# Moving one stage six steps later, reordering four loads, and giving the last stores more buffers and a second queue

## The chip, the cores and the metric

The kernel runs on one core of a Trainium2 chip. The metric is the device time of one execution in microseconds (us), as the median of several runs. A profile (a trace of one execution) exists of every kernel named here; its span is about 2 us shorter than the time of the same run. Engines: PE is the matmul engine, ACT, DVE and POOL (GpSimd) are the elementwise engines, SP only issues DMAs here.

## The reference

A filter in the frequency domain, then a gated feed-forward network (FFN) on the result:

```python
# x (8, 3008, 256); filt_r, filt_i (1505, 256); w_gate, w_val (256, 1536); w_out (1536, 256)
X = np.fft.rfft(x, axis=1)
y = np.fft.irfft(X * (filt_r + 1j * filt_i)[None], n=3008, axis=1)
t = y.reshape(24064, 256)
out = (np.maximum(t @ w_gate, 0) * (t @ w_val)) @ w_out
```

## The kernel before

The Fourier transform is factored, 3008 = 94 x 32, and done by matmuls in stages for each of eight batches:

- stage A: `psA` from x, written as `asb` to DRAM (`Abuf`, four stores), read back in another order as `at` (four loads);
- stage B: `psX` from `at`, times the filter, `psD`, written to DRAM (`Dbuf`), read back as `dC` (eight loads, z = 0 to 7; call them D loads);
- stage C: `psY` from `dC` into `yT`, the input of the FFN.

The FFN has 47 blocks of 512 tokens with 12 steps each. A step makes `psV` and `psG` (four matmuls, 0.86 us together) and, for the block before, a third of a 128-row tile of `psO` (four matmuls, 0.43 us), so about 1.30 us. The stages of the next batch are put between the steps, at step numbers that the program gives. Batch 0 has nothing to hide behind; it is the prologue, about 63 us.

```python
def load_at(b, c):                                    # SP queue
    ...
    nc.sync.dma_start(ats[b][32 * c:32 * c + 32], ... Abuf[b] ...)

def load_d(b, z0=0, z1=NZ):                           # SP queue
    for z in range(z0, z1):
        dC = sb.tile([NROW, 4, D], BF16, tag="dC", bufs=12)
        nc.sync.dma_start(dC, ... Dbuf[b] ...)
...
    last = blk == NB - 1                              # o_part: psO and the output
    if s in (5, 11) or last and s % 3 == 2:
        t0 = t if last else t - 1
        osb = fs.tile([128, 2, D], FP32, tag="osb", bufs=3)
        nc.scalar.copy(osb[...], psO[...])
        for tt in range(t0, t + 1):
            for (o, b, n2, n1, w) in runs(blk * W + tt * 128, 128):
                nc.sync.dma_start(_ap(out, ..., [[N2 * D, w], [1, D]]), osb[o:o + w, tt % 2])
...
for f in items_b(0, amid): f()                        # end of the prologue
load_d(0, 0, 2)
... # WvT, WgT, WoT: the rest of the FFN's weights, by POOL
for i in range(8): next(early)()                      # stage A of batch 1, 12 of its 16 parts now done
for h in range(2): item_c(0, h)
load_d(0, 2)                                          # six more D loads
...
C_AT = (8, 10)                                        # stage C of the next block in each block
for b in range(1, B):
    s0, sb0 = (0, 13) if b == 1 else ...              # first step of stage A, of stage B
    ...
        at_step(... if b > 1 else 4, lambda b=b, c=c: load_at(b, c))
    for i, f in enumerate(items_b(b)):
        at_step(sb0 + 2 * i, f)
    at_step(sb0 + 27, lambda b=b: load_d(b))
```

A tile of 128 token rows is scattered in DRAM: `runs` cuts it where a row of the 94 x 32 grid ends, so its store is two or three DMAs of, say, 94 and 34 rows of 1 KB each.

## Time and profile before

985.33 us, median of three runs (983.27 to 986.04); the profiled span is 982.2 us.

The profile's page, engines' busy time and the chain of waits (the work that ended last, followed backwards):

```profile
PE 951.0 (97%) x6020; PEld 565.2 (58%) x6020; DVE 544.9 (55%) x823; ACT 526.7 (54%) x940; POOL 42.9 (4%) x76
PE 91%; DMA 5%; SPq 1%; ACT 0%; issue 0%; DVE 0%; POOL 0%; ACTq 0%; POOLq 0%
```

PE bounds this kernel. A change that leaves PE's instructions alone can win only its holes, so the next view is what PE waited for. Columns: who waited, the producer, total us, how often, the longest.

```profile
PE psX L274 <- DMA at<-Abuf: 16.3, 3, 8.2
...
PE psO L373 <- ACT osb L379: 2.5, 2, 2.0
...
PE psG L355 <- DMA WgT<-in_moe_w_gate_dram: 1.3, 1, 1.3
```

Of the 16.3 us, 8.2 are in the prologue and 0.8 near 338 us. The rest is one hole of 7.33 us, seen in PE's timeline (start, duration, what; in brackets the idle time before it and who ended it):

```profile
81.63 0.60 PE L373 MATMUL psO<-WoT,prod 128*128 128x256 bf16 x4
89.55 0.61 PE L274 MATMUL psX<-at,F 128*128 128x256 bf16 x2 [7.33 <-DMA at<-Abuf]
89.95 1.06 PE L355 MATMUL psV<-yT,WvT 128*128 128x512 bf16 x2
```

The psV after the hole takes 1.06 us instead of 0.59. The view of stretches of time says why: the last three numbers of each line are the granted clock, the DMA share and GB/s, and the clock is 0.50. (The DMA share is the summed time of the packets over that of 16 engines. Packets overlap, so it can pass 1.)

```profile
82.00:89.50 7.50, 0.23 (x3) 0.00 (x0) 0.69 (x1) 0.00 (x0) 0.00 (x0) 0.76 0.91 141
89.50:92.50 3.00, 2.95 (x10) 1.49 (x11) 1.81 (x3) 0.59 (x1) 2.42 (x6) 0.50 0.38 98
```

What the `at` load waited for is on SP's timeline: the last Abuf store of stage A leaves at 71.67, behind six D loads.

```profile
63.18 8.39 SPq L317 DMA_DIRECT2D dC<-Dbuf  x6
71.67 1.60 SPq L247 DMA_DIRECT2D Abuf<-asb  x1
73.38 8.78 SPq L261 DMA_DIRECT2D at<-Abuf  x4
```

Last, the tail in the chain of waits: a store holds an `osb` buffer, ACT waits for it, PE waits for ACT and then runs its last 12 matmuls at half clock.

```profile
968.76 3.94 DMA out_dram<-osb
...
972.88 0.38 ACT osb L379
973.26 0.04 issue
973.30 2.69 PE psO L373 x12
```

The end of the run in the view of stretches matters later. But for one short copy on ACT only the DMA engines work, and they only little: a share of 0.14 or 0.15 is about two of 16, at about 50 GB/s.

```profile
976.20:978.20 2.00, 0.00 (x0) 0.00 (x0) 0.00 (x0) 0.23 (x1) 0.00 (x0) 0.50 0.14 48
978.20:980.20 2.00, 0.00 (x0) 0.00 (x0) 0.00 (x0) 0.00 (x0) 0.00 (x0) 0.50 0.15 51
```

### The profile page before, as it was taken

What the parts mean: (1) busy time and instruction counts of PE and PEld (TensorE: products, weight loads), DVE (VectorE), ACT (ScalarE), POOL (GpSimd) and SP (SyncE); (2) the same over time, 40 slices, a digit from 0 to 9 for tenths busy, and PEclk for the clock granted to TensorE, in tenths of its full rate; (3) what the DMA queues carried; (4) which work ended last, traced back from release to release, by engine and by line L of the source; (5) the groups of instructions that cost most, each with busy time, mean ns of one, the idle gap of its engine ahead of it and who ended that gap; (6) DMA issues with size and microseconds to landing.
All of it is one profiled execution on the core that took longest, in us unless ns stands there. A gap on an engine that the chain in (4) does not pass through costs nothing.

```text
span 982.2 us, 16279 instructions
## 1 busy us (share of the span) xinstructions
PE 951.0 (97%) x6020; PEld 565.2 (58%) x6020; DVE 544.9 (55%) x823; ACT 526.7 (54%) x940; POOL 42.9 (4%) x76
## 2 busy tenths in 40 slices
PE   8696999999999999999999999999999999999996
PEld 3343666556664566556665566655666556666664
DVE  2635865348653576536854377543775348655552
ACT  4463555555555555555555555555555555555552
POOL 4221000010000100001000010000100000000000
PEclk9798999999999999999999999999999999999998
DMA  9989241243243442345241362423614241241111
GB/s 261 241 223 236 85 117 38 78 127 144 79 98 94 123 148 80 73 102 199 64 125 46 94 199 80 113 56 102 189 57 113 71 107 44 80 98 34 33 33 44
DMA packets 94432, 106.29 MB, mean 108 GB/s; under 512 B 7796, under 2 KB 84724, under 8 KB 92660
## 3 DMA queue, kind: packets, MB, share of 16 engines
q1 hardware_dynamic: 87520, 80.03, 30.5%
q0 software_dynamic: 6240, 22.71, 7.8%
q10 hardware_dynamic: 592, 2.51, 0.7%
q8 instruction: 47, 0.77, 0.4%
q14 instruction: 33, 0.27, 0.1%
HBM read 59.32 MB, written 49.81 MB: 111 GB/s over the span
## 4 chain that ended last, share of the span: by engine, by line
PE 91%; DMA 5%; SPq 1%; ACT 0%; issue 0%; DVE 0%; POOL 0%; ACTq 0%; POOLq 0%
PE psO L373 24%; PE psV L355 24%; PE psG L355 24%; PE psA L242 10%; DMA Abuf<-asb 3%; PE psX L274 2%; PE psY L339 2%; PE psD L294 2%; PE psD L293 2%; DMA at<-Abuf 2%; SPq L317 1%; PE psJ L392 1%; DMA out_dram<-osb 0%; ACT asb L245 0%; POOL uu L281 0%
## 5 line engine op out<-in xcount | busy, mean ns | idle before, releaser
L360 DVE SCALAR_TENSOR_TENSOR prod<-psG,vsb 128x512 bf16<-128x512 f32 x564 | 390.1, 692 | 370.4 <-ACT vsb L358 358.4
L358 ACT CAST vsb<-psV 128x512 bf16<-128x512 f32 x564 | 331.2, 587 | 223.3 <-PE psV L355 192.5
L373 PE MATMUL psO<-WoT,prod 128*128 128x256 bf16 x2256 | 338.5, 274 | 2.5 <-ACT osb L379 2.5
L355 PE MATMUL psG<-yT,WgT 128*128 128x512 bf16 x1128 | 335.8, 379 | 1.3 <-DMA WgT<-in_moe_w_gate_dram 1.3
L355 PE MATMUL psV<-yT,WvT 128*128 128x512 bf16 x1128 | 336.2, 379 | 0.8 <-ACT yT L344 0.6
L373 PEld LDWEIGHTS <-prod 128*128 128x128 bf16 x2256 | 221.4, 98 | 147.1 <-issue 3.4
L355 PEld LDWEIGHTS <-WgT 128*128 128x128 bf16 x1128 | 110.0, 98 | 135.8 <-DMA WgT<-in_moe_w_gate_dram 1.8
L355 PEld LDWEIGHTS <-WvT 128*128 128x128 bf16 x1128 | 104.4, 98 | 59.9 <-issue 49.7
L242 PE MATMUL psA<-XF,WA 128*96 128x512 f32 x256 | 129.5, 592 | 0.0
L245 ACT CAST asb<-psA 96x512 bf16<-96x512 f32 x128 | 74.2, 582 | 102.2 <-PE psA L242 97.7
L296 ACT CAST dsb<-psD 128x512 bf16<-128x512 f32 x96 | 56.1, 587 | 52.6 <-PE psD L294 51.1
L277 DVE TENSOR_TENSOR tt<-psX,Ftr 128x512 bf16<-128x512 f32 x96 | 65.4, 682 | 16.4 <-PE psX L274 15.9
L379 ACT COPY osb<-psO 128x512 f32<-128x512 f32 (+1 forms) x96 | 55.4, 577 | 33.3 <-PE psO L373 27.8
L283 DVE TENSOR_TENSOR uu<-psX,Fti 128x512 bf16<-128x512 f32 x90 | 61.3, 681 | 0.0
L274 PE MATMUL psX<-at,F 128*128 128x256 bf16 x192 | 38.1, 283 | 16.3 <-DMA at<-Abuf 16.3
L294 PE MATMUL psD<-uu,I2u 128*128 128x256 bf16 x192 | 48.2, 278 | 1.6 <-POOL uu L281 1.5
L293 PE MATMUL psD<-tt,I2t 128*128 128x256 bf16 x192 | 48.4, 278 | 0.0
L339 PEld LDWEIGHTS <-dC 96*128 96x128 bf16 x604 | 34.6, 97 | 13.2 <-issue 11.1
L346 DVE CAST yT<-psY 128x512 bf16<-128x512 f32 x47 | 32.1, 684 | 16.4 <-PE psY L339 16.4
L242 PEld LDWEIGHTS psA<-XF,WA 128*96 128x96 f32 x256 | 35.1, 163 | 9.3 <-ACT asb L245 4.0
L344 ACT CAST yT<-psY 128x512 bf16<-128x512 f32 x47 | 27.5, 586 | 19.6 <-PE psY L339 19.5
L339 PE MATMUL psY<-M,dC 96*128 96x94 bf16 (+18 forms) x604 | 37.5, 198 | 0.0
(45 smaller groups left out, 154.9 us busy)
## 6 DMA issues: line engine op xcount, KB each, us to landing
XF<-in_x_dram POOLq DMA_DIRECT2D x34, 512.0 KB, 6.2
Abuf<-asb SPq DMA_DIRECT2D x32, 384.0 KB
at<-Abuf SPq DMA_DIRECT2D x32, 384.0 KB
dC<-Dbuf SPq DMA_DIRECT2D x64, 192.0 KB
Dbuf<-dsb SPq DMA_DIRECT2D x31, 384.0 KB
out_dram<-osb SPq DMA_DIRECT2D x72, 94.0 KB
XF<-in_x_dram SPq DMA_DIRECT2D x8, 512.0 KB
tabs<-dft_tab ACTq DMA_DIRECT2D x2, 576.0 KB
```

The costliest lines, as they stand in the source:

```text
L242: nc.tensor.matmul(psA[0:NROW], WA[:, :NROW], XF[c * NC2 // NX2][:, o:o + 512], start=True, stop=True)
L245: nc.scalar.copy(dst, psA[0:NROW])
L274: nc.tensor.matmul(psX[:, i], F2[:, g + i, :], at[:, g + i, :], start=True, stop=True)
L277: nc.vector.tensor_tensor(tt, psX, Ftr[:, g:g + 2, :], op=ALU.mult)
L283: nc.vector.tensor_tensor(uu, psX, Fti[:, g:g + 2, :], op=ALU.mult)
L293: nc.tensor.matmul(psD[:, i], I2t[:, g + i, :], tt[:, i], start=True, stop=False)
L294: nc.tensor.matmul(psD[:, i], I2u[:, g + i, :], uu[:, i], start=False, stop=True)
L339: nc.tensor.matmul(psY[:, o:o + w], dCs[b, n2 // 4][:, n2 % 4, h * 128:(h + 1) * 128], M1[:, n1:n1 + w], start=True, stop=True)
L355: nc.tensor.matmul(pt[:, :W], w[:, h, ft * 128:(ft + 1) * 128], yt[:, h, :], start=(h == 0), stop=(h == 1))
L358: nc.scalar.copy(vsb, psV[:, :W])
L360: nc.vector.scalar_tensor_tensor(prod, in0=psG[:, :W], scalar=0.0, in1=vsb, op0=ALU.max, op1=ALU.mult)
L373: nc.tensor.matmul(psO[:, t % 2], prods[ft][:, t * 128:(t + 1) * 128], WoT[:, ft, :], start=(ft == 0), stop=(ft == NFT - 1))
```

## The change

The intent: stage B of batch 1 starts when its data are there; the D loads that are not needed yet leave the road to the Abuf store and the `at` loads; the tail no longer waits for an output buffer; two engines issue the last stores.

```diff
-                st["dsb"] = sb.tile([128, GC, D], BF16, tag="dsb", bufs=5, name="dsb")
+                st["dsb"] = sb.tile([128, GC, D], BF16, tag="dsb", bufs=4, name="dsb")
...
-            osb = fs.tile([128, 2, D], FP32, tag="osb", bufs=3)
+            osb = fs.tile([128, 2, D], FP32, tag="osb", bufs=5)
...
-                for (o, b, n2, n1, w) in runs(blk * W + tt * 128, 128):
-                    nc.sync.dma_start(_ap(out, ...), osb[o:o + w, tt % 2])
+                for i, (o, b, n2, n1, w) in enumerate(runs(blk * W + tt * 128, 128)):
+                    eng = nc.scalar if last and i == 1 else nc.sync
+                    eng.dma_start(_ap(out, ...), osb[o:o + w, tt % 2])
...
-    load_d(0, 2)
+    load_d(0, 2, 4)
...
+    for s, z in ((9, 4), (14, 6)):
+        at_step(s, lambda z=z: load_d(0, z, z + 2))
     C_AT = (8, 10)
     for b in range(1, B):
-        s0, sb0 = (0, 13) if b == 1 else (end - 54, end - 30 | 1)
+        s0, sb0 = (0, 19) if b == 1 else (end - 54, end - 30 | 1)
...
-            at_step(s0 + n - 10 + 4 * c if b > 1 else 4, lambda b=b, c=c: load_at(b, c))
+            at_step(s0 + n - 10 + 4 * c if b > 1 else 5, lambda b=b, c=c: load_at(b, c))
```

More of the change, by code (lines that the diff above doesn't have):

```diff
@@ L377, in o_part @@
             t0 = t if last else t - 1
-            osb = fs.tile([128, 2, D], FP32, tag="osb", bufs=3)
+            osb = fs.tile([128, 2, D], FP32, tag="osb", bufs=5)
             nc.scalar.copy(osb[:, t0 % 2:t % 2 + 1], psO[:, t0 % 2:t % 2 + 1])
             for tt in range(t0, t + 1):
-                for (o, b, n2, n1, w) in runs(blk * W + tt * 128, 128):
-                    nc.sync.dma_start(_ap(out, (b * S + n1 * N2 + n2) * D, [[N2 * D, w], [1, D]]),
-                                      osb[o:o + w, tt % 2])
+                for i, (o, b, n2, n1, w) in enumerate(runs(blk * W + tt * 128, 128)):
+                    eng = nc.scalar if last and i == 1 else nc.sync
+                    eng.dma_start(_ap(out, (b * S + n1 * N2 + n2) * D, [[N2 * D, w], [1, D]]),
+                                  osb[o:o + w, tt % 2])
     junk = pro.tile([128, 512], BF16, tag="junk", bufs=1)
```

## The prediction

> **What bounds the kernel now.** The page gives PE 951.0 of 982.2 us busy (97%), and the chain of waits is 91% PE. From 92.5 to 966 us PE is full but for 0.79 us near 338, so only PE's holes can be won. PE's waits and timeline place those that the change can touch:
>
> 1. A hole of 7.33 us, 82.2 to 89.55: psX waits for `at`, the last quarter of batch 1's stage A. SP issues in order: six D loads of batch 0 hold it from 63.18 to 71.57 us, so the last Abuf store, whose ACT copy ended at 71.0, goes out at 71.67, lands after 9.91 us (DMA share 0.9 to 1.0), and its `at` load takes 7.86 us more. A later batch has 7.7 + 4.3 us there and a stall of 0.79 us.
> 2. After the hole the granted clock is 0.50 from 89.5 to 92.5; that costs 1.5 us. The Trainium skill (TensorE: Matmul & The Clock Gate, "The HAM clock gate") has half rate after an idle window of about 3.4 us; the trace agrees.
> 3. 1.29 us at 71 where psG waits for WgT, which shares the DMA engines with the D loads.
> 4. The tail: psO of the last tile waits 2.04 us for the osb copy before it, which waits for an output DMA (3.94 us) as all three osb buffers are in use. Then its 12 matmuls take 2.57 us at half clock instead of 1.3.
>
> **What the change does.** Only two D loads (0.39 MB, not 1.18 MB) stand before the last Abuf store; the order listing shows the other four behind the `at` loads on SP. Stage B starts 6 steps later, 6 x 1.30 = 7.8 us. PE's instructions are the same. Five osb buffers remove the tail wait. The second piece of each last tile is issued by ACT, about 0.3 us each as on SP (estimate), between copies 1.3 us apart.
>
> **Sum.** 0.79 MB less at the 205 GB/s of 55 to 95 us is 3.8 us, so `at` lands at 85 to 86 us. PE reaches its first psX at 88.7 to 90. Item 1 vanishes: -7.3, item 2 with it: -1.5. WgT comes earlier: -1.0. Tail: last psO ends 3.1 us sooner, parallel issue 0.3. Total -13.2.
>
> New waits: z=4 of batch 0 is needed by psY at step 20, about 1.5 us after stage B starts, and is issued behind the last `at` load; I expect it at 87 to 88, a margin of 2 to 3 us. Batch 1's D loads come at step 46 for use at step 56; other batches live with 8 steps. Four dsb buffers: batch 0's fifth use takes the first one again, stored at 45 and wanted at 55; no or a short ACT wait. I allow +0.7 for these.
>
> 985.3 - 13.2 + 0.7 = 972.8 us; range 969.5 to 977.5. Faster by over 2% (under 965.6) 0.02, within 2% 0.97, slower 0.01.
>
> **Right if:** psX <- at falls from 16.3 us to about 9 (8.15 in the prologue stays), the clock is 1.0 through 80 to 95, the pair Abuf and `at` near 70 us shrinks or leaves the chain, psO <- osb copy falls from 2.5 to about 0.5, span near 970.
>
> **Wrong if:** `at` still lands after 90 us because Abuf's 9.9 us is congestion by weights, not D loads; psY waits for dC at steps 20 or 56; ACT's DMA issues cost over 1 us each; dsb reuse stalls the prologue; or the final store's landing, not its issue, grows.

## The result, and the profile after

976.29 us, median of four runs (975.31 to 976.92), against 985.35 us (the three runs of before above and one more). The ratio of the mean time of the changed kernel's runs to that of the kernel before in the same rounds is 0.9911, 95% interval 0.9894 to 0.9928 (so it is not quite the ratio of the medians). The time was inside the predicted range, 3.5 us above the predicted 972.8.

PE's waits after. The 0.5 in the osb line is the longest; the other at<-Abuf wait, of 1.4 us, is near 331 us.

```profile
PE psX L274 <- DMA at<-Abuf: 9.3, 2, 7.9
...
PE psG L355 <- DMA WgT<-in_moe_w_gate_dram: 2.2, 1, 2.2
...
PE psO L373 <- ACT osb L379: 0.9, 2, 0.5
```

The hole is gone, and so is the half clock after it. In the timeline of PE psX follows psO without a gap, and the same stretches of time are at clock 1.00:

```profile
89.83 0.60 PE L373 MATMUL psO<-WoT,prod 128*128 128x256 bf16 x4
90.26 0.38 PE L274 MATMUL psX<-at,F 128*128 128x256 bf16 x2
```

```profile
82.00:89.50 7.50, 7.45 (x47) 4.60 (x47) 3.98 (x6) 3.80 (x7) 1.77 (x5) 1.00 0.94 166
89.50:92.50 3.00, 3.00 (x27) 1.94 (x25) 2.45 (x5) 1.44 (x3) 1.57 (x4) 1.00 1.07 361
```

SP's timeline after: the Abuf store leaves 1.1 us sooner, as soon as its data are there, with two D loads before it and four behind the `at` loads.

```profile
62.71 1.13 SPq L317 DMA_DIRECT2D dC<-Dbuf  x2
70.56 0.31 SPq L247 DMA_DIRECT2D Abuf<-asb  x1
70.97 7.45 SPq L261 DMA_DIRECT2D at<-Abuf  x4
78.47 6.50 SPq L317 DMA_DIRECT2D dC<-Dbuf  x4
```

The tail is another matter. ACT's timeline after: the copies (COPY osb) and the stores that ACT issues. The copy of 963.30 is done at 963.67, but its store goes out at 964.71; the last copy is done at 965.60, its store goes out at 967.08.

```profile
963.30 0.37 ACT L379 COPY osb<-psO 128x256 f32<-128x256 f32 x1 [0.94 <-PE psO L373]
964.71 0.33 ACTq L383 DMA_DIRECT2D out_dram<-osb  x1
965.23 0.37 ACT L379 COPY osb<-psO 128x256 f32<-128x256 f32 x1 [1.56 <-DMA out_dram<-osb]
967.08 0.24 ACTq L383 DMA_DIRECT2D out_dram<-osb  x1
```

The chain of waits names what the first of the two waited for: a store that SP issued at 960.04 and that landed 4.59 us later.

```profile
960.04 4.59 DMA out_dram<-osb
964.63 0.02 issue
964.66 0.02 ACTq L383
```

And the end of the run is as empty as before, DMA share 0.12 to 0.19:

```profile
968.90:970.90 2.00, 0.00 (x0) 0.00 (x0) 0.00 (x0) 0.00 (x0) 0.00 (x0) 0.68 0.19 63
970.90:972.90 2.00, 0.00 (x0) 0.00 (x0) 0.00 (x0) 0.00 (x0) 0.00 (x0) 0.50 0.12 43
```

Cutting both profiled runs at three events that both have (read off PE's timeline) says where the time went:

| stretch | before, us | after, us | difference |
|---|---|---|---|
| start to the first psV (prologue) | 63.33 | 62.87 | -0.46 |
| first psV to the last psG | 902.34 | 894.81 | -7.53 |
| last psG to the end of the last psO | 10.31 | 7.52 | -2.79 |
| end of the last psO to the end | 6.22 | 9.70 | +3.48 |
| span | 982.2 | 974.9 | -7.3 |

The whole tail, from the last psG on, went from 16.53 to 17.22 us. PE finished 2.8 us sooner, and the wait for the stores took it back. (The profiled runs differ by 7.4 us in time, 984.35 and 976.92; the medians by 9.1. The profiled run of after was the slowest of its four. The total PE busy time is not compared: 110 of 6020 matmul records are missing in the second trace.)

Two questions were put to the chip. Which of the early parts, the delay or the order of the D loads, closed the hole? And why did the tail give nothing?

### The profile page after: what moved, and what is told of

It reads as the page before. It is cut to its first block, busy times and chain, and to the rows that moved or that the text cites. A ratio compares the mean times of both kernels' runs of the same rounds, so it can differ in the third digit from the quotient of the medians. Undisturbed runs are those within 1.5% of the kernel's fastest.

```text
span 974.9 us, 16167 instructions
## 1 busy us (share of the span) xinstructions
PE 942.0 (97%) x5910; PEld 564.1 (58%) x6020; DVE 544.3 (56%) x823; ACT 526.7 (54%) x940; POOL 43.0 (4%) x76
## 4 chain that ended last, share of the span: by engine, by line
PE 89%; DMA 5%; ACT 1%; DVE 1%; issue 1%; POOL 0%; ACTq 0%; SPq 0%; POOLq 0%
PE psG L355 24%; PE psO L373 24%; PE psV L355 23%; PE psA L242 9%; DMA Abuf<-asb 2%; PE psX L274 2%; PE psD L294 2%; PE psD L293 2%; PE psY L339 2%; DMA WgT<-in_moe_w_gate_dram 1%; DMA at<-Abuf 1%; DVE prod L360 1%; ACT vsb L358 1%; PE psJ L393 1%; DMA out_dram<-osb 1%
## 5 line engine op out<-in xcount | busy, mean ns | idle before, releaser
L355 PE MATMUL psG<-yT,WgT 128*128 128x512 bf16 x1096 | 328.4, 379 | 5.8 <-DMA WgT<-in_moe_w_gate_dram 2.2
L355 PE MATMUL psV<-yT,WvT 128*128 128x512 bf16 x1051 | 319.0, 379 | 1.6 <-ACT yT L344 0.6
L339 PEld LDWEIGHTS <-dC 96*128 96x128 bf16 x604 | 34.5, 97 | 13.2 <-issue 10.8
```

Source lines behind the costliest of these rows:

```text
L339: nc.tensor.matmul(psY[:, o:o + w], dCs[b, n2 // 4][:, n2 % 4, h * 128:(h + 1) * 128], M1[:, n1:n1 + w], start=True, stop=True)
L355: nc.tensor.matmul(pt[:, :W], w[:, h, ft * 128:(ft + 1) * 128], yt[:, h, :], start=(h == 0), stop=(h == 1))
```

## The experiments

Each was timed against the kernel before in the same rounds. All were correct. The columns "FFN" (first psV to last psG), "PE's end" (last psG to the end of the last psO) and "stores" (from there to the end) are read from each profile as in the table above; "tail" is the sum of the last two. The medians of before in the same rounds were 985.31 us (e1, e2, e3, e9), 984.94 (e4, e6, e7, e8) and 984.93 (g1, g2, g3, f1).

| run | median us | ratio to before | FFN | PE's end | stores | tail |
|---|---|---|---|---|---|---|
| before | 985.33 | 1 | 902.34 | 10.31 | 6.22 | 16.53 |
| after | 976.29 | 0.9911 | 894.81 | 7.52 | 9.70 | 17.22 |
| e1_late_only | 975.26 | 0.9898 | 892.96 | 10.73 | 6.50 | 17.23 |
| e2_dorder_only | 982.66 | 0.9972 | 900.24 | 9.06 | 7.62 | 16.68 |
| e3_no_tail | 975.93 | 0.9902 | 893.78 | 9.49 | 7.66 | 17.15 |
| e9_weights_split | 976.88 | 0.9909 | 894.39 | 7.51 | 9.68 | 17.19 |
| e4_one_queue | 974.64 | 0.9888 | 893.10 | 7.51 | 9.04 | 16.55 |
| e6_split_one_queue | 972.79 | 0.9870 | 893.19 | 7.51 | 6.66 | 14.17 |
| e7_split_two_queues | 973.30 | 0.9875 | 893.20 | 10.61 | 4.19 | 14.80 |
| e8_pool_queue | 973.20 | 0.9875 | 893.54 | 7.51 | 6.91 | 14.42 |
| g1_after_again | 976.22 | 0.9903 | 893.40 | 7.52 | 9.72 | 17.24 |
| g2_late_again | 975.89 | 0.9904 | 893.22 | 9.53 | 7.57 | 17.10 |
| g3_one_queue_again | 974.69 | 0.9896 | 892.73 | 7.51 | 8.97 | 16.48 |
| f1_late_split | 971.41 | 0.9856 | 893.66 | 7.51 | 5.74 | 13.25 |

The 95% intervals are about plus or minus 0.0016 wide (0.0020 for f1_late_split), 1.6 us. Differences below that rest on the traces, where a stretch of the tail repeats within 0.1 us for the same code of the changed kernel (17.22 and 17.24; 16.55 and 16.48).

### e1_late_only: the delay alone

```diff
# against before
-        s0, sb0 = (0, 13) if b == 1 else ...
+        s0, sb0 = (0, 19) if b == 1 else ...
```

> Before with stage B of batch 1 six steps later and nothing else. Theory L (the delay alone closes the hole, since the at load of before lands at 89.5 us and PE reaches its psX at about 90): psX waits for at no more than 0.5 us near 90, the clock stays 1.0 through 80 to 95, about 976.5 us (985.3 less 7.3 less 1.5). Theory O (the order of the D loads is needed too, as the prediction had it): a hole of 2 us or more is left, 979 us or more.

975.26 us. (What the program counts from the first step of stage B moves with it: batch 1's D loads and batch 2's loads of x.) PE's waits show no hole at batch 1: at<-Abuf is 8.3 us in all, of which 7.5 are in the prologue and 0.8 at a later batch. `at` is there by 88.70 us, when POOL, which waits for the same data, goes on; PE reaches its psX at 89.08, with no idle time before it:

```profile
88.70 0.18 POOL L226 CAST scr<-at 32x8 f32<-32x8 bf16 x1 [27.01 <-DMA at<-Abuf]
89.08 0.38 PE L274 MATMUL psX<-at,F 128*128 128x256 bf16 x2
```

Theory L holds. The time is as good as the whole change's, with the six D loads still in the way, though with only 0.4 us to spare (0.3 in the second trace of this kernel, g2). In the changed kernel POOL goes on at 87.28 and PE reaches psX at 90.26: the new order of the D loads bought about 2.6 us of margin, but no time.

### e2_dorder_only: the order alone

```diff
# against before
-    load_d(0, 2)
+    load_d(0, 2, 4)
+    for s, z in ((9, 4), (14, 6)):
+        at_step(s, lambda z=z: load_d(0, z, z + 2))
-            ... if b > 1 else 4, lambda b=b, c=c: load_at(b, c))
+            ... if b > 1 else 5, lambda b=b, c=c: load_at(b, c))
```

> Before with four D loads moved behind the at loads and nothing else. The prediction had at land 3.8 us earlier: hole of 3.5 us left, about 981.5 us. The trace of after has at 2.3 us earlier (87.2 instead of 89.5): hole of about 5 us, 983 us, clock still falling to half after it. If D loads were all of the congestion: hole under 2 us, under 979 us.

982.66 us, 2.8 us less than before by the ratio (0.0028 of 985). PE's timeline still has the hole, 2.15 us shorter, and the slow psV after it:

```profile
82.21 0.60 PE L373 MATMUL psO<-WoT,prod 128*128 128x256 bf16 x4
87.99 0.59 PE L274 MATMUL psX<-at,F 128*128 128x256 bf16 x2 [5.18 <-DMA at<-Abuf]
88.37 1.06 PE L355 MATMUL psV<-yT,WvT 128*128 128x512 bf16 x2
```

So 0.79 MB of D loads out of the way brings `at` about 2.2 us sooner, not the 3.8 that bytes over mean rate gave. (That counts from the first psV, which is 0.55 us later in this trace; on the trace's own clock it is 1.6.) The DMA engines stay as busy as before (share 1.10 at 64 to 66 us and 1.26 at 70 to 72, against 1.03 and 1.26), with POOL's weight loads and SP's loads and stores; that these are what holds up the rest of the path is argued, not shown.

### e3_no_tail: both early parts without the tail part

```diff
# against after
-                st["dsb"] = ... bufs=4
+                st["dsb"] = ... bufs=5
-            osb = ... bufs=5
+            osb = ... bufs=3
-                    eng = nc.scalar if last and i == 1 else nc.sync
+                    eng = nc.sync
```

> After without its tail part (three osb buffers, all stores on SP, five dsb buffers). The prediction had the tail worth 3.4 us: this would take about 979.7 us. The theory from the trace of after (last psO to the end grew by about as much as PE gained): tail worth 0 to 1 us, this 975.5 to 977.3 us, and from the last psG to the end of the span 16.5 us as before.

975.93 us, within the expected range: the tail part of the change was worth nothing. Its tail is 17.15 us, a little over the expected 16.5. The tail of this code (three buffers, SP alone) varies between 16.5 and 17.2 us in five traces (before, e1, e2, e3, g2); the split between PE's end and the stores varies more, 9.1 to 10.7 against 6.2 to 7.7. Most of the difference in PE's end is the clock of its last 12 matmuls: they took 2.7 us at half clock in before and e1, and 1.47 us at full clock in e2, e3 and g2. PE may end early or late, and the end of the run hardly moves.

### e9_weights_split: the weights in two column ranges

```diff
# against after
-    load_vg(DFF // 3, DFF)
+    load_vg(DFF // 3, DFF // 2)
+    load_vg(DFF // 2, DFF)
```

> After with the second load of WvT and WgT cut into two column ranges, the earlier needed first. Theory W (psG of step 4 waits because a whole 0.5 MB WvT load stands before its own columns): the wait of 2.2 us at 70 to 72 vanishes or falls below 0.5, and the time by about 2 us, to 974.2. Rival (the DMA engines are saturated and whatever is asked for comes at 72): the wait stays between 1.5 and 3 us, the time within 1 us of after, or the shorter pieces (256 columns) cost more than they gain and later weights are waited for.

976.88 us: no gain, as the rival had it. PE's waits show the wait for WgT at 1.0 us and a new one of 1.3 us of psO for WoT, which comes later now:

```profile
PE psO L373 <- DMA WoT<-in_moe_w_out_dram: 1.3, 1, 1.3
PE psG L355 <- DMA WgT<-in_moe_w_gate_dram: 1.0, 1, 1.0
```

The 2.2 us of the first profile of the changed kernel were a chance: the same kernel again (g1) waited 1.3 us, and other kernels with the same loads between 0.5 and 1.3.

### e4_one_queue: all stores on SP

```diff
# against after
-                    eng = nc.scalar if last and i == 1 else nc.sync
+                    eng = nc.sync
```

> After with all stores on SP (five osb buffers stay). Theory T (the tail ends when stores of few rows in parallel have landed; who issues them does not matter): from last psG to the end within 1 us of after's 17.2 us, time within 1 us of 976.3. Rival Q (stores on ACT are what lengthened the end): 3 us less from last psG to the end, about 973.3 us. Prediction: two queues save 0.3 us, so 976.6.

974.64 us. The tail is 16.55 us, 0.67 less than with two queues. So the second queue costs something, but it isn't the 3 us that rival Q asked for: PE ends at 7.51 as in the changed kernel, and the stores still take 9.04 us. Theory T, that it is the landing of the stores that ends the run, stands.

The packed trace shows it directly: it keeps each rise of a store's completion semaphore, which no view prints. In e4 the last store (94 rows) is issued 8.36 us after the last psG, against 11.07 in the kernel before, and is complete 15.4 us after it in both: the 2.7 us went into a landing of 7.05 us in place of 4.36. In e4 the stores of 86, 94, 34 and 94 rows complete one after another, at 966.79, 968.85, 970.56 and 972.56 us, although all were issued by 965.51.

Why ACT's stores went out late is in the listing of the built program, which names the semaphores that each instruction waits for. The DMAs issued by SP and ACT share eight completion semaphores in this program, DMAHW0 to DMAHW7, taken in turn. The listing of the changed kernel's last instructions on ACT, then on SP (cut to the stores):

```
ACT  out_dram<-osb 86x256 [waits DMAHW2_49,Activation_49]
ACT  out_dram<-osb 94x256 [waits DMAHW6_49,Activation_49]
ACT  out_dram<-osb 60x256 [waits DMAHW1_49,Activation_49]
ACT  out_dram<-osb 94x256 [waits DMAHW3_49,Activation_49]
SP   out_dram<-osb 94x256 [waits DMAHW0_49]
SP   out_dram<-osb 18x256 [waits DMAHW1_49]
SP   out_dram<-osb 76x256 [waits DMAHW3_49]
...
SP   out_dram<-osb 34x256 [waits DMAHW4_49,Activation_49]
```

ACT's store of 60 rows waits for semaphore 1, which SP's store of 18 rows holds: the one issued at 960.04 that landed 4.59 us later. ACT's last store waits for semaphore 3, by the listing that of SP's 76 rows; in the packed trace that store is complete at 967.00, and ACT's goes out at 967.08. So a DMA of this program is not only issued in its queue's order; it also waits for the DMA eight before it, whether SP or ACT issued that one. Issuing from both doesn't help against this.

### e6_split_one_queue: stores of a multiple of 16 rows

The end of the run has a DMA share of about two engines of 16, and 94, 86 and 34 rows are each twice a prime. The Trainium skill (DMA: Bandwidth & Descriptors, "Why a DMA increments its semaphore by 16 and not by 1", the paragraph "How many engines") says that such a DMA is spread over the largest number up to 16 that divides its slowest dimension, here the rows: 2 for 94, 86 and 34, 4 for 76 and 68. So the wide stores of the last block were cut.

```diff
# against after
-                    eng = nc.scalar if last and i == 1 else nc.sync
-                    eng.dma_start(_ap(out, (b * S + n1 * N2 + n2) * D, [[N2 * D, w], [1, D]]),
-                                  osb[o:o + w, tt % 2])
+                    eng = nc.sync
+                    w0 = w // 16 * 16 if last and w % 16 and w > 63 or last and w == 34 else w
+                    for (o1, w1) in ((0, w0), (w0, w - w0)):
+                        if w1:
+                            eng.dma_start(_ap(out, (b * S + (n1 + o1) * N2 + n2) * D,
+                                              [[N2 * D, w1], [1, D]]),
+                                          osb[o + o1:o + o1 + w1, tt % 2])
```

> After with all stores on SP, and the stores of the last block of 86, 94, 68 and 34 rows cut into a piece of a multiple of 16 rows and the rest. Theory E (a store of 94 or 86 rows is moved by two of the 16 DMA engines, as the DMA share of 0.13 at the end of before suggests): the last stores land 2 to 4 us sooner, from last psG to the end 13 to 15 us, about 973 us. Rival S (semaphores: each of eight serves every eighth DMA, and more DMAs wait more): same or longer than one queue unsplit.

972.79 us, and the tail is 14.17 us, 2.4 less than uncut on one queue, all of it in the landing of the stores. Theory E holds, and rival S, that more DMAs wait longer for semaphores, falls: a DMA that lands sooner also gives its semaphore back sooner.

The packed trace has the number of engines, too, if each late rise of a store's semaphore is one engine's end. In the last block of the changed kernel the semaphore rises once at issue and then, as data land, 2 times for each store of 94, 86 and 34 rows, 4 times for 76 and 68, 13 for 52 and 26; in e6 it rises 16 times for 80, 64 and 32. These are the rule's numbers. The last cut stores of e6 (80 and 14 rows, issued at 967.04 and 967.42) are complete after 2.1 and 1.9 us. No run cut the stores into pieces that stay on two engines, so that more pieces alone would not do is argued, from the stores of e4 that land one after another.

The stretches of the end show more engines at work, and at the very end none:

```profile
964.60:966.60 2.00, 0.00 (x0) 0.00 (x0) 0.00 (x0) 0.00 (x0) 0.00 (x0) 1.00 0.25 72
966.60:968.60 2.00, 0.00 (x0) 0.00 (x0) 0.00 (x0) 0.00 (x0) 0.00 (x0) 0.69 0.28 82
968.60:970.60 2.00, 0.00 (x0) 0.00 (x0) 0.00 (x0) 0.00 (x0) 0.00 (x0) 0.50 0.00 1
```

### e7_split_two_queues: the cut stores on two queues

```diff
# against e6_split_one_queue
-                    eng = nc.sync
+                    eng = nc.scalar if last and i == 1 else nc.sync
```

> The same cut with the second piece's stores on ACT as in after. Theory E: as the split on one queue, within 1 us. If the issue of DMAs is now the limit: 0.5 to 1 us less than on one queue.

973.30 us, no gain over one queue, and the trace shows the harm of the second queue better than the changed kernel did. ACT issues in order, so a store that waits for its semaphore holds the next copy behind it. In ACT's timeline two stores, begun at 962.41, hold ACT until 965.05; the copy after them starts at 965.17:

```profile
962.41 2.64 ACTq L386 DMA_DIRECT2D out_dram<-osb  x2
965.17 0.37 ACT L379 COPY osb<-psO 128x256 f32<-128x256 f32 x1 [2.79 <-DMA out_dram<-osb]
```

PE waited 2.3 us for that copy and then ran at half clock (10.61 us instead of 7.51): the stall that the five buffers had removed is back by another way.

### e8_pool_queue: the second pieces on GpSimd

```diff
# against after
-                    eng = nc.scalar if last and i == 1 else nc.sync
+                    eng = nc.gpsimd if last and i == 1 else nc.sync
```

> After with the second pieces of the last block issued by GpSimd instead of ACT, uncut. Its DMAs have semaphores of their own, so nothing waits for a store eight before. Theory S (the wait for a semaphore is the loss): the last store goes out within 1 us of its copy, from last psG to the end 13 to 15 us. Theory E would give the same if GpSimd's queue spreads 94 rows over more engines, to be read from the DMA share (above 0.13); if its share stays low, the end stays near 17 us. So together with the split runs it separates the two only if one of them fails.

973.20 us, tail 14.42 us. GpSimd's stores go out as their copies end (the last at 965.79) and land fast: the profile's list of DMA issues gives 2.8 us in the median for the two stores of 94 rows (5.0 for the one of 86). The DMA share is 0.62 at 962 to 964 us and 0.38 at 964 to 966, so the spread is there too; as the expectation said, this run alone can't tell semaphores from spread, and e6 decides that the spread is worth 2.4 us. The DMA engines are nearly idle from 968 us on (share 0.01), yet the run ends at 972.0. In every other run here the last DMA completes 1.0 to 1.7 us before the end; in this one it is 4.0. What it does in those 4 us (the chain has GpSimd's own closing instruction there) stays open.

### The last four, with more rounds

> The changed kernel again, to be compared within the same rounds with the next three. 976.3 us as at first (ratio 0.991); if the first profile was a fair one, the tail from last psG to the end is 17.2 us again, with ACT issuing its last store over 1 us after the copy it waits for.

> Only stage B six steps later, again. Theory (the delay is the whole gain, the D order and the tail part are worth nothing together): equal to the changed kernel within 1 us or faster by up to 1.5 us. The prediction's sum had it slower by 3.4 us, the tail.

> The changed kernel with all stores on SP, again. Theory (ACT's stores wait for one of eight semaphores that SP's earlier stores hold, and the second queue gives nothing back): faster than the changed kernel by 0.5 to 2 us. Rival (the queue does not matter and the first difference of 1.6 us was between two chip jobs): within 0.4 us.

In the same rounds the changed kernel took 976.22 us, the delay alone 975.89 and the changed kernel with one queue 974.69. The first two are equal: ratios 0.9903 and 0.9904. So the delay is all of the change's gain that can be measured. The one queue is 1.5 us faster by the medians and 0.7 us by the ratios (0.9896), with intervals that overlap; the traces have the tail at 17.24 and 16.48 us, as the first time. I take the cost of the second queue to be about 0.7 us, shown by the traces and not by the times.

f1_late_split takes what worked: the delay, five `osb` and four `dsb` buffers, one queue, D loads in their old place, and cut stores in the last two blocks.

```diff
# against before
-    tag="dsb", bufs=5   /   tag="osb", bufs=3   /   s0, sb0 = (0, 13)
+    tag="dsb", bufs=4   /   tag="osb", bufs=5   /   s0, sb0 = (0, 19)
+                    cut = blk >= NB - 2 and (w > 63 or w == 34)
+                    w0 = w // 16 * 16 if cut else w
+                    for (o1, w1) in ((0, w0), (w0, w - w0)):
+                        if w1:
+                            nc.sync.dma_start(...)      # rows o1 to o1 + w1, as in e6_split_one_queue
```

> Before with stage B six steps later, five osb and four dsb buffers, all stores on SP, and the wide stores of the last two blocks cut into a multiple of 16 rows and the rest; D loads in their old place. Theory: delay 8.9 us and tail 2 to 4 us, about 972 us, the fastest of all; from last psG to the end 13 to 14 us, with the DMA share never near 0.13 for several us.

971.41 us, 13.5 us less than the median of before in the same rounds (984.93) and 14.2 us less by the ratio 0.9856, and the fastest of all. Its tail is 13.25 us; the DMA share is 0.30, 0.24 and 0.14 in the last six us. The last 0.14 is not two engines as in before: all stores are complete at 968.65, in the middle of that stretch.

```profile
963.70:965.70 2.00, 0.26 (x3) 0.00 (x0) 0.00 (x0) 0.37 (x1) 0.00 (x0) 1.00 0.30 82
965.70:967.70 2.00, 0.00 (x0) 0.00 (x0) 0.00 (x0) 0.00 (x0) 0.00 (x0) 0.92 0.24 72
967.70:969.70 2.00, 0.00 (x0) 0.00 (x0) 0.00 (x0) 0.00 (x0) 0.00 (x0) 0.50 0.14 43
```

## Why the prediction was right or wrong

The time lay in the range, as its sum was right in its two largest terms. Point by point:

- "Item 1 vanishes: -7.3, item 2 with it: -1.5." Right: no hole, clock 1.00 in 82 to 95 us, and the FFN's stretch shrank by 7.5 us with two small losses inside it (WgT +0.9, a later batch's `at` +0.65). The Trainium skill's half rate after about 3.4 us of idling (TensorE: Matmul & The Clock Gate, "The HAM clock gate") fits the two long holes: after 7.33 and 5.18 us matmuls ran at half rate, and the full rate came back after about 3 us. It does not settle the shorter waits of the tail: after 2.04 us (before), 2.31 (e7) and 2.43 (e1) the last 12 matmuls ran at half clock, after 2.00 (e2), 2.43 (e3) and 2.48 (g2) at full. What decides there is not shown.
- "0.79 MB less at the 205 GB/s of 55 to 95 us is 3.8 us." The term was mis-sized: e2 measured 2.15 us of hole. And it was not needed: e1 closed the hole without it. The prediction had 88.7 to 90 for PE and knew 89.55 for the old `at`; it could have seen that the delay alone might just suffice.
- "WgT comes earlier: -1.0." Wrong: +0.9 in the first profile, 0 in the second. Fewer D loads did not bring the weights sooner.
- "Tail: last psO ends 3.1 us sooner, parallel issue 0.3." The first half happened, 2.8 us. The step that failed is that it would shorten the run by as much. The end is set by the landing of stores of 94, 86 and 34 rows on about two DMA engines, and PE's 2.8 us turned into 3.5 us more of waiting for them (on one queue, e4, the last store went out 2.7 us sooner and took 2.7 us longer to land); the second queue took about 0.7 us instead of giving 0.3. The prediction's own list had it ("the final store's landing, not its issue, grows"), with no weight in the sum. With the measured +0.7 for the tail in place of -3.4 the sum is -13.2 + 3.4 + 0.7 = -9.1, and the medians differ by 9.1; as the WgT term and a later batch's `at` were off too, that closeness is partly luck.
- New waits: none of those named came in the first profile. No psY waited for a D load, and the four dsb buffers stalled nothing that PE waited for. Their +0.7 was not needed.

## What to carry to other kernels

With PE full, removing a wait in the middle was worth its whole length and the half clock after it; but ending PE's work sooner was worth nothing as the last stores landed when they did, so read the DMA share in the last microseconds first. Here a share near 2/16, while stores were under way, meant that their shape and not their queue set the end: try giving the last stores a row count with a large divisor up to 16. A wait at a fixed place in an interleaved program is most cheaply closed by moving the consumer later, if its own consumers have slack.

## What the Trainium skill lacked or had wrong

- No page has it: DMAs issued by SP and ACT in this program share eight completion semaphores in turn, so that a store on ACT waited for an unrelated one on SP (issued at 960.04, landed 4.59 us later; the store went out 1.04 us after its copy, the last one 1.48 us), and a copy behind such a store waited 2.79 us (e7).
- DMA: Bandwidth & Descriptors, "Issuing engines are not separate DMA queues", says that issuing from several engines saves only the sequencer's issue time. The runs agree that there is no gain and add a cost: the tail was 17.22 and 17.24 us with two queues, 16.55 and 16.48 with one.
- The same page's rule of how many engines serve a DMA agrees with a DMA share of 0.14 to 0.15 at the end of before and with the 2.4 us won by cut stores; it does not say what this means for the last stores of a kernel. The packed trace agrees with the number (2 late rises of the semaphore for 94, 86 and 34 rows, 4 for 76 and 68, 16 for 80). It does not keep which engine moved which packet, so that the engines are the same two for each store is not shown; the stores of e4 landing one after another fit it.
- No page that I read explains the 4 us at the end of the run whose last stores GpSimd issued, with a DMA share of 0.01 and 0.00 (last DMA complete 4.0 us before the end, 1.0 to 1.7 in the other runs).
